# Moving four small reciprocal deviations from ScalarE to Pool in a fused attention and GEGLU kernel

## The chip, the cores and the metric

The kernel runs on one core of a Trainium2 chip. A core has a matmul engine (TensorE, PE in the profile, with its weight loads as PEld), three engines for element-wise work (VectorE as DVE, ScalarE as ACT, GpSimd as POOL) and a sync engine (SP) that issues most DMA transfers. Each engine runs its own queue of instructions in order; an instruction waits on semaphores for what other engines or transfers must have done before it.

The metric is the device time of one execution in microseconds, less is better. The kernel before takes 213.56 us, the median of 3 runs that lie between 213.23 and 213.91 us.

## The reference

The input is one sequence of 2048 rows with 448 columns in bf16. A layer norm without weights feeds two branches, sliding-window attention (16 heads of 28 columns, window 256) and a gated feed-forward layer of width 1792. Their outputs are added to the input.

```python
def _layernorm(x, axis=-1, eps=1e-5):
    m = jnp.mean(x, axis=axis, keepdims=True)
    v = jnp.var(x, axis=axis, keepdims=True)
    return (x - m) / jnp.sqrt(v + eps)

xn = _layernorm(x, axis=-1)
return x + _A_ref(xn, A_wqkv, A_wo) + _B_ref(xn, B_w_gate, B_w_up, B_w_down)
```

The attention branch is a QKV product, masked scores with softmax, the product with V, and the output product with `wo`. The feed-forward branch is `(gelu(x @ w_gate) * (x @ w_up)) @ w_down`.

## The kernel before, in words

The 2048 rows are 16 tiles of 128 rows, one row per partition. Four tiles form a block of 512 rows (`QB`), and the main loop runs over four blocks (`NB`). In each block the scores, their exponentials (L657) and the products with V are interleaved, by a plan written out by hand, with feed-forward products (L457, L391), projections for the next block (L319, L333) and the statistics of later tiles. The order of instructions on each engine is the order of the Python calls (`manual_schedule`); no scheduler moves them.

What the change touches lies ahead of the loop, in the layer norm of the first four tiles. For a tile t:

- `stat(t)` (L155, L156) computes mean and variance of each row on VectorE (`bn_stats`, then the short `bn_aggr`) into `mv_all[:, t, :]`.
- `rstd(t, n)` (L160, L161) turns the variances of n tiles into reciprocal standard deviations in `rstd_all`. It does so on ScalarE in two instructions, Ln of variance plus eps into the work tile `lnv`, then Exp with scale -0.5. One table of ScalarE, loaded at the start (L135), holds both functions and also serves the softmax.
- `norm(t)` (L170) subtracts the mean and multiplies by `rstd_all` on VectorE, giving the bf16 tile `xn`.
- `transp(t, copy, tag)` (L185, L186) transposes it by four small matmuls into the PSUM bank named by `tag`, and copies the result into `xnT`. Tiles 0 and 2 use bank b2, tiles 1 and 3 bank b3; the copies of tiles 0, 1 and 2 run on ScalarE, that of tile 3 on VectorE.

The calls stand in this order (other calls between them left out), and this gives the order of each engine's queue:

```python
warmup(9)
stat(0); rstd(0, 1); stat(1); rstd(1, 1); norm(0)
stat(2); rstd(2, 1); transp(0, nc.scalar.copy, "b2"); norm(1)
stat(3); rstd(3, 1); warmup(1); transp(1, nc.scalar.copy, "b3")
v_dense(0, pvs[0])
norm(2); transp(2, nc.scalar.copy, "b2"); norm(3)
pads(nc.vector.tensor_copy, wqp, slice(0, 1))
transp(3, nc.vector.tensor_copy, "b3")
```

`warmup(n)` (L150) issues n matmuls on zeros (the tile `warm`, cleared by VectorE at L124), which keep PE running while the first loads arrive. `v_dense` (L190) is the dense part of the V product of one tile. Behind the lines shown follow Pool's copy of the last columns of `xnT` (L739), a weight copy on ScalarE (L712), `v_dense(1)`, and the first Q and K products (L190 into `s`), which read all four tiles of `xnT`; then Pool builds the masks (`make_masks`, L117), and VectorE begins tile 4.

Ahead of all this Pool clears two parts of the V tile (L103, L104). `rstd` is called for tile 4, for tiles 5 to 7 together, for 8 to 11 and for 12 to 15 as well. The work tile `lnv` has three buffers in turn.

Of the kernel before, what the change touches and what calls it, by code (L numbers as in the profile page):

```python
# [10 lines left out]
ALU = mybir.AluOpType  # L11
AX = mybir.AxisListType
bf16 = mybir.dt.bfloat16
f32 = mybir.dt.float32
# [3 lines left out]
P = 128  # L18
# [9 lines left out]
def kernel(  # L28
# [11 lines left out]
    nc = tc.nc  # L40
    const = ctx.enter_context(tc.tile_pool(name="const", bufs=1))
# [78 lines left out]

    eps_t = const.tile([P, 1], f32, name="eps_t")
    nc.vector.memset(eps_t[:, :], 1e-5)
    warm = wo[:, :, :].rearrange("p g n -> p (g n)")
    nc.vector.memset(warm[:, 0:QB], 0.0)  # L124
    wqp = const.tile([P, 3, H, 32], bf16, name="wqp")
# [17 lines left out]
    mv_all = const.tile([P, NT, 2], f32, name="mv_all")  # L143
    rstd_all = const.tile([P, NT], f32, name="rstd_all")
# [12 lines left out]

    def rstd(t, n):
        lnv = work.tile([P, 4], f32, name="lnv")
        nc.scalar.activation(out=lnv[:, 0:n], in_=mv_all[:, t:t + n, 1], func=ACT.Ln, bias=eps_t[:, 0:1], scale=1.0)  # L160
        nc.scalar.activation(out=rstd_all[:, t:t + n], in_=lnv[:, 0:n], func=ACT.Exp, scale=-0.5)  # L161

# [555 lines left out]
    warmup(9)  # L718
    stat(0)
    rstd(0, 1)  # L720
    stat(1)
    rstd(1, 1)
    norm(0)
    stat(2)
    rstd(2, 1)
    transp(0, nc.scalar.copy, "b2")
    norm(1)
# [300 lines left out]
```

## Time and profile before

| | |
|---|---|
| median of the runs | 213.56 us |
| the profiled execution, its own time | 213.22 us |
| its span, first to last instruction | 211.5 us |
| mean granted clock of TensorE | 1.000 |
| instructions | 6340 |

The profile is of one execution, and its times count from the span's start. A line of its timeline has start, length, engine, line of the kernel, operation, what it writes and reads, shapes and the number of instructions merged in it; in brackets stands the idle time of the engine ahead of it and what ended it. A line of the chain has start, length, engine and tile. The chain follows the work that ended last back from the end, at each step to what released it. A matmul's length includes its passage through the array, so matmuls in a row overlap and their starts say more than their lengths. Lengths on Pool are rough.

### The profile page before, as it was taken

The page shows a single profiled execution, that of the slowest core. Times are in us where ns is not written, and L with a number is a line of the kernel's source. Part 1 is how long each engine was busy: PE and PEld are TensorE (multiplying, and loading weights), DVE is VectorE, ACT ScalarE, POOL GpSimd, SP SyncE. Part 2 cuts the span into 40 slices and gives each one's busy share as a digit, 9 for nine tenths or more (in the row PEclk, how much of TensorE's full clock was granted, in tenths as well). Part 3 has the DMA queues.
Part 4 walks back from the last instruction along what each step waited for, and adds up shares of the span by engine and source line. Part 5 has one row for each costly group of instructions (what it writes and reads, how often), then busy time and mean ns, then how long its engine had stood idle before and what let it go on. Part 6 is the DMA issues. An engine that isn't in the chain of part 4 may idle for free.

```text
span 211.5 us, 6340 instructions
## 1 busy us (share of the span) xinstructions
PE 206.6 (98%) x2682; PEld 97.4 (46%) x2682; DVE 156.8 (74%) x355; ACT 131.6 (62%) x123; POOL 48.9 (23%) x86
## 2 busy tenths in 40 slices
PE   7999999999999999999999999999999999999994
PEld 2333444444454545444445444544444454544562
DVE  6899988999767985696437897395384699659722
ACT  4699488566677977413778787523577786757000
POOL 5388658451100220041000112013000022005100
PEclk9999999999999999999999999999999999999999
DMA  6999989969410101003521000100100011000011
GB/s 167 289 236 203 108 212 221 220 189 223 111 47 29 39 11 34 9 4 67 74 75 47 25 0 27 22 0 16 31 3 0 10 41 41 7 3 0 22 60 39
DMA packets 24889, 15.67 MB, mean 74 GB/s; under 512 B 9208, under 2 KB 24728, under 8 KB 24856
## 3 DMA queue, kind: packets, MB, share of 16 engines
q1 hardware_dynamic: 23814, 14.87, 32.3%
q8 instruction: 22, 0.36, 0.7%
q10 hardware_dynamic: 1042, 0.34, 0.7%
q14 instruction: 11, 0.09, 0.2%
HBM read 9.26 MB, written 2.41 MB: 55 GB/s over the span
## 4 chain that ended last, share of the span: by engine, by line
PE 94%; DVE 2%; ACT 1%; DMA 1%; issue 0%; DVEq 0%; ACTq 0%
PE po L391 24%; PE gt L457 20%; PE u L457 12%; PE ue L457 8%; PE pq L333 7%; PE sc L653 7%; PE ov L625 5%; PE pv L319 4%; PE pq L190 2%; PE pl L391 2%; DVE st L155 1%; DMA x_sb<-in_A_x_dram 1%; PE pv L190 1%; ACT p_sb L657 1%; PE s L190 1%; PE pk L190 1%
## 5 line engine op out<-in xcount | busy, mean ns | idle before, releaser
L657 ACT ACTIVATE p_sb<-sc 128x2048 bf16<-128x2048 f32 x39 | 73.2, 1878 | 20.6 <-PE sc L653 14.4
L497 ACT ACTIVATE p_sb<-gt 128x1024 bf16<-128x1024 f32 x28 | 28.7, 1024 | 33.7 <-PE gt L457 30.7
L592 POOL TENSOR_TENSOR oN<-oc,l 128x512 bf16<-128x512 f32 x16 | 21.6, 1354 | 119.0 <-DVE l L605 119.0
L457 PE MATMUL gt<-xnT,wg 64*128 64x512 bf16 x224 | 45.6, 376 | 0.0
L391 PE MATMUL po<-wd,hT 128*128 128x448 bf16 x210 | 43.3, 353 | 0.0
L457 PE MATMUL gt<-xsw,wg 64*128 64x512 bf16 x168 | 40.7, 376 | 0.0
L505 DVE TENSOR_TENSOR hT<-p_sb,u 128x512 bf16<-128x512 bf16 x34 | 21.9, 677 | 16.0 <-PE u L457 15.8
L573 DVE TENSOR_TENSOR p_sb<-p_sb,masks 128x256 bf16<-128x256 bf16 (+1 forms) x90 | 27.8, 364 | 7.6 <-ACT p_sb L657 7.6
L391 PEld LDWEIGHTS <-hT 128*128 128x128 bf16 x238 | 21.9, 98 | 19.4 <-issue 2.2
L457 PEld LDWEIGHTS <-wg 64*128 64x128 bf16 x392 | 19.0, 94 | 22.5 <-issue 0.2
L457 PEld LDWEIGHTS <-wu 64*128 64x128 bf16 x392 | 18.8, 94 | 22.4 <-issue 1.0
L457 PE MATMUL u<-xnT,wu 64*128 64x512 bf16 x136 | 28.1, 376 | 0.0
L457 PE MATMUL u<-xsw,wu 64*128 64x512 bf16 x102 | 24.7, 376 | 0.0
L457 PE MATMUL ue<-xnT,wu 64*128 64x512 bf16 x88 | 18.0, 377 | 0.0
L381 DVE TENSOR_TENSOR res<-po,x_sb 128x448 bf16<-128x448 f32 x15 | 9.0, 619 | 11.5 <-PE po L391 11.0
L653 PE MATMUL sc<-qT,kT 28*64 28x320 bf16 (+7 forms) x648 | 16.4, 261 | 0.1
L457 PE MATMUL ue<-xsw,wu 64*128 64x512 bf16 x66 | 16.3, 377 | 0.0
L583 POOL TENSOR_SCALAR_AFFINE_SELECT p_sb<-p_sb 128x512 bf16<-128x512 bf16 (+1 forms) x21 | 14.2, 705 | 5.9 <-ACT p_sb L657 5.8
L610 DVE TENSOR_TENSOR oc<-oc,ov 128x512 f32<-128x512 f32 x12 | 8.2, 681 | 8.6 <-ACT oc L609 8.6
L653 PEld LDWEIGHTS <-kT 28*64 28x64 bf16 (+1 forms) x648 | 7.5, 102 | 13.3 <-issue 12.0
L474 DVE CAST hT<-ue 128x512 bf16<-128x512 f32 x18 | 11.6, 679 | 1.8 <-PE ue L457 1.8
L391 PE MATMUL po<-wo,oN 128*128 128x448 bf16 x54 | 12.0, 352 | 0.0
(110 smaller groups left out, 278.9 us busy)
## 6 DMA issues: line engine op xcount, KB each, us to landing
out_dram<-res SPq DMA_DIRECT2D x15, 112.0 KB
wd<-in_B_w_down_dram SPq DMA_DIRECT2D x2, 784.0 KB
x_sb<-in_A_x_dram SPq DMA_DIRECT2D x3, 448.0 KB
xsw<-xnT SPq DMA_DIRECT2D x6, 192.0 KB
wu<-in_B_w_up_dram SPq DMA_DIRECT2D x4, 224.0 KB
wg<-in_B_w_gate_dram SPq DMA_DIRECT2D x2, 448.0 KB
wu<-in_B_w_up_dram SPq DMA_DIRECT2D x2, 336.0 KB
wg<-in_B_w_gate_dram SPq DMA_DIRECT2D x2, 336.0 KB
```

Of the source, the lines that this page charges most:

```text
L190: nc.tensor.matmul(ps, lhsT=lhs(c), rhs=rhs(c), start=start and c == 0, stop=stop and c == 2, skip_group_check=True)
L333: nc.tensor.matmul(ps, lhsT=w.rearrange("p h d -> p (h d)"), rhs=xchunk(qb, hi, c, qb * QB, QB), start=c == 0, stop=c == 6, tile_position= ...
L391: nc.tensor.matmul(po[:, 0:w], lhsT=x[:, k, tt * P:(tt + 1) * P], rhs=wt[:, k, lo:up], start=start and n == 0, stop=stop and n == len(term ...
L457: nc.tensor.matmul(ps, lhsT=w[64 * hi:64 * hi + 64, c, p * P:(p + 1) * P], rhs=xchunk(qb, hi, c, qb * QB, QB), start=c == 0, stop=c == 6, ...
L474: copy(out=hTs[qb][:, p + 7 * i, :], in_=us[i])
L497: nc.scalar.activation(out=ges[p][:, :, :], in_=gt[:, :, :], func=ACT.Gelu_apprx_tanh)
L505: nc.vector.tensor_tensor(out=hT[:, p + 7 * i, :], in0=ge[:, i, :], in1=u, op=ALU.mult)
L573: nc.vector.tensor_tensor(out=reg, in0=reg, in1=m, op=ALU.mult)
L583: nc.gpsimd.affine_select(out=reg, in_=reg, pattern=mid + [[1 if diag else -1, min(w, P)]], compare_op=ALU.is_ge, fill=0.0, base=0 if diag ...
L592: nc.gpsimd.tensor_tensor(out=oN[:, g, :], in0=oc[:, :], in1=inv, op=ALU.mult)
L653: nc.tensor.matmul(ss[k0:k0 + nk, j, col:col + nq], lhsT=kT[r, g, kt * P + k0:kt * P + k0 + nk], rhs=qT[r, g, ring(qb).start + q0:ring(qb) ...
L657: nc.scalar.activation(out=p_sb[:, :, 0:ncol], in_=ss[:, :, 0:ncol], func=ACT.Exp, scale=SCALE)
```

## The change

For the first four tiles the reciprocal deviation is computed by Pool in two instructions: variance plus eps into `lnv`, then that to the power of a tile that holds -0.5. The tile is cleared to this value by a new memset on VectorE, between those of `eps_t` and `warm`. For tiles 4 to 15 ScalarE's Ln and Exp remain, and its table is loaded as before.

```diff
     eps_t = const.tile([P, 1], f32, name="eps_t")
     nc.vector.memset(eps_t[:, :], 1e-5)
+    minus_half = const.tile([P, 1], f32, name="minus_half")
+    nc.vector.memset(minus_half[:, :], -0.5)
...
     def rstd(t, n):
         lnv = work.tile([P, 4], f32, name="lnv")
+        if t < 4:
+            nc.gpsimd.tensor_scalar(out=lnv[:, 0:n], in0=mv_all[:, t:t + n, 1], scalar1=1e-5, scalar2=None, op0=ALU.add)
+            nc.gpsimd.tensor_tensor(out=rstd_all[:, t:t + n], in0=lnv[:, 0:n], in1=minus_half[:, 0:n], op=ALU.pow)
+            return
         nc.scalar.activation(out=lnv[:, 0:n], in_=mv_all[:, t:t + n, 1], func=ACT.Ln, bias=eps_t[:, 0:1], scale=1.0)
         nc.scalar.activation(out=rstd_all[:, t:t + n], in_=lnv[:, 0:n], func=ACT.Exp, scale=-0.5)
```

On Pool the eight new instructions stand behind the two memsets of the V tile (L103, L104) and ahead of the copy of L739. On ScalarE the eight old ones are gone from ahead of and between the copies of L186. PE's and SP's instructions and their order are the same.

## The prediction

> **What bounds the kernel now.** I read the page's busy shares first, then the waits, then the chain of waits over the first 9 us, since all four replaced pairs lie there.
>
> ```profile
> span 211.5 us, 6340 instructions
> PE 206.6 (98%) x2682; PEld 97.4 (46%) x2682; DVE 156.8 (74%) x355; ACT 131.6 (62%) x123; POOL 48.9 (23%) x86
> ...
> PE wps L150 <- DVE wo L124: 1.4, 1, 1.4
> PE pv L190 <- ACT xnT L186: 0.4, 1, 0.4
> ```
>
> The first two lines are the page's. The last two are every idle stretch that the view of waits gives PE over the first 30 us, and the same view of the whole span has no more of them: 1.42 us until the first warm-up matmul and 0.36 us before the first V product. From there on PE is the bound, and a shift of its start at 8.6 us reaches the end nearly one for one. So the question is whether the start shifts. Lines of the chain there (start, length, work):
>
> ```profile
> 3.58 0.18 DVE mv_all L156
> ...
> 6.38 0.20 DVE mv_all L156
> ...
> 6.60 0.30 ACT lnv L160
> ...
> 6.93 0.20 ACT rstd_all L161
> 7.13 0.48 ACT xnT L186
> ...
> 7.65 0.38 PE tp L185 x4
> ```
>
> Up to 6.58 it runs on VectorE through the statistics of one tile after the other; of ScalarE's pairs only the fourth tile's, 6.60 to 7.13, lies on it. The timeline of the two engines (start, length, engine, line, and idle time in brackets) shows why:
>
> ```profile
> 3.81 0.29 ACT L160 ACTIVATE lnv<-mv_all,eps_t 128x1 f32<-128x1 f32 x1
> 4.14 0.20 ACT L161 ACTIVATE rstd_all<-lnv 128x1 f32<-128x1 f32 x1
> 4.41 0.36 DVE L170 TENSOR_SCALAR xn<-x_sb,mv_all,rstd_all 128x448 bf16<-128x448 bf16 x1
> ...
> 6.00 0.57 ACT L186 COPY xnT<-tp 128x512 bf16<-128x512 bf16 x1
> 6.48 0.37 DVE L170 TENSOR_SCALAR xn<-x_sb,mv_all,rstd_all 128x448 bf16<-128x448 bf16 x1
> 7.04 1.17 ACT L186 COPY xnT<-tp 128x512 bf16<-128x512 bf16 x2
> 7.16 0.40 DVE L170 TENSOR_SCALAR xn<-x_sb,mv_all,rstd_all 128x448 bf16<-128x448 bf16 x1 [0.32 <-ACT rstd_all L161]
> 7.20 0.84 PE L185 MATMUL tp<-ident,xn 128*128 128x128 bf16 x8
> 8.08 0.42 DVE L186 COPY xnT<-tp 128x512 bf16<-128x512 bf16 x1 [0.33 <-PE tp L185]
> 8.56 0.82 PE L190 MATMUL s<-xnT,wqp 128*128 128x512 bf16 x3
> ```
>
> Call X the time from the end of a tile's aggregate to the start of its norm, as far as the pair sets it. For tile 0 the norm could start at 3.76 + 0.65 = 4.41 without moving; tiles 1 and 2 have more room, since VectorE's next statistics lie in between. Tile 3 has none: aggregate done at 6.56, norm at 7.16, X = 0.60, VectorE idle 0.32 us. Behind that norm stand its transposes (7.65), VectorE's copy (8.08) and the Q product (8.56), which needs all four tiles. So X of tile 3 is paid in full, and X of tile 0 from 0.65 on is paid a second time, because tiles 1 to 3 queue behind norm 0 on VectorE.
>
> **The change part by part.** ScalarE loses four pairs of 0.29 + 0.20 us. Its first copy, held until 6.00 by the third pair, can follow the transposes, and its second, now 7.04, can start near 6.3. PE gains nothing by either: the first V product may start some 0.4 us earlier, but PE's order then has the transposes of tiles 2 and 3, and tile 3's wait for norm 3. Today the freed bank (second copy done at 7.61) and norm 3 (7.56) release it together, so with the copy earlier norm 3 alone decides, 0.03 us sooner. That is ScalarE's whole contribution, a gain of 0.03.
>
> Pool gains two instructions per tile, in its queue behind the two memsets of the V tile and ahead of the copy at 8.67:
>
> ```profile
> 1.01 0.06 DVE L122 MEMSET eps_t<- 128x1 f32 x1
> ...
> 2.92 0.63 DVE L155 BATCH_NORM_STATS2 st<-x_sb 128x6 f32<-128x448 bf16 x1 [0.90 <-DMA x_sb<-in_A_x_dram]
> ...
> 1.42 3.94 PE L150 MATMUL wps<-wo 128*128 128x512 bf16 x9 [1.42 <-DVE wo L124]
> 5.20 0.39 PE L185 MATMUL tp<-ident,xn 128*128 128x128 bf16 x4
> 5.87 0.40 PE L185 MATMUL tp<-ident,xn 128*128 128x128 bf16 x4
> ...
> 2.14 1.52 POOL L104 MEMSET v_sb<- 128x768 bf16 x1
> 8.67 0.61 POOL L739 COPY xnT<-xnT 64x512 bf16<-64x512 bf16 x1 [5.01 <-ACT wkp L712]
> ```
>
> Pool is free from 3.66, before the first aggregate at 3.76, and idle for 5.01 us: nothing that is queued behind the new waits is wanted before tile 3's copy (8.50), which comes after the last new instruction. The added memset of the exponent costs 0.06 us on VectorE, inside its 0.90 us wait for the first tile. It delays the warm-up matmuls by as much; the nine end near 5.36 and tile 0's transposes start at 5.20 among them, but nobody waits for these before tile 1's at 5.87. Nothing there; 0.06 if that cover were gone. No DMA is added or moved.
>
> Now the price of a Pool pair. Rows for small Pool instructions and for how Pool is woken (by line and form: busy, mean ns; by line: min/median/max ns; the timeline):
>
> ```profile
> L283 POOL COPY wqp<-wraw 128x16 bf16<-128x16 bf16 x3 | 0.6, 190 | 0.0
> L1012 POOL MEMSET const-float32-0.0<- 128x1 f32 x1 | 0.1, 103 | 0.3 <-issue 0.3
> ...
> L592 POOL TENSOR_TENSOR oN<-oc,l x16: 1264/1270/1719, 32.8 to 194.3; 128x512 bf16<-128x512 f32 x16
> ...
> L117 POOL TENSOR_SCALAR_AFFINE_SELECT masks<-masks x18: 232/237/359, 9.3 to 14.3; 64x64 bf16<-64x64 bf16 x18
> ...
> 76.06 0.70 DVE L605 STREAM_TRANSPOSE l<-inv_all 128x512 f32<-128x512 f32 x1
> 76.85 1.27 POOL L592 TENSOR_TENSOR oN<-oc,l 128x512 bf16<-128x512 f32 x1 [4.84 <-DVE l L605]
> ...
> 12.61 0.38 DVE L170 TENSOR_SCALAR xn<-x_sb,mv_all,rstd_all 128x448 bf16<-128x448 bf16 x1
> 12.71 0.36 POOL L117 TENSOR_SCALAR_AFFINE_SELECT masks<-masks 64x64 bf16<-64x64 bf16 x1
> ```
>
> Wake by VectorE: 76.76 to 76.85, so 0.08 to 0.09. The addition is nearest to the 16-column copy: 0.19. Between dependent instructions 0.04, as between ScalarE's two (4.10 to 4.14). From Pool to VectorE I take the same 0.04. The addition of tiles 1 to 3 starts while VectorE runs the norm of the tile before (6.48 to 6.85 against 6.64). A mask instruction that started 0.10 us into a norm took 0.36 in place of the median 0.237: 0.12 more. A gain by such a neighbour is excluded.
>
> The Trainium skill says the same more sharply in "SBUF — State Buffer", section "SBUF: two separate sides": whichever of a GpSimd instruction and a VectorE one in a two-port mode starts first holds the shared port pair to its end, and the other is fully blocked. By that rule the addition of tile 3 would run only after 6.85 and end at 7.04, against 6.95 by the row: 0.09 more in the sum. The row agrees that there is a charge, but the mask instruction ended 0.08 after the norm, not its own 0.237.
>
> The power p has no row. Lower end: the 128x1 memset, 0.10. Upper end: a whole two-input instruction of 512 columns, 1.27. One column is nearest to the small rows, 0.19, but a general power is more work per column than a copy, so I take 0.45, a quarter of the way from 0.19 to 1.27.
>
> Sum with p: X of tile 0 is 0.08 + 0.19 + 0.04 + p + 0.04 = 0.35 + p, of tile 3 with the neighbour's 0.12 it is 0.47 + p. At p = 0.45: norm 0 is late by 0.80 - 0.65 = 0.15, norm 3 by a further 0.92 - 0.60 = 0.32, less the 0.03 of the freed bank: **+0.44 us** (in general 2p - 0.46 for p above 0.30, and p - 0.16 below). Against the profiled execution, 213.22 us with 1.7 us outside its span, that is 213.66; that execution is 0.34 under the median of the runs, so 214.0 by the median, 0.2% up. A measurement of this kernel cannot tell 0.3%, 0.64 us, from no change.
>
> **The rivals.**
>
> *A pair no slower than ScalarE's.* With both instructions at the memset's 0.11 and no neighbour's charge, X is 0.38, norm 3 starts at 6.94, and the gain is 0.22 + 0.03 = 0.25: 213.3. More than about 0.34 is not there, since norm 2 ends at 6.85 and VectorE's 0.32 us of idling is all that tile 3 can give back. For it: Pool idles there, and the chain shows ScalarE's pair. Against it: two instructions at 0.19 with the wake already make 0.54 before any power is computed.
>
> *The power is slow and Pool becomes the chain (slower).* Place: the four pairs in Pool's queue. It decides beyond noise from p = 0.55, where 2p - 0.46 reaches 0.64, and from about p = 0.72 the pairs wait for each other. At p = 1.27 the four take 4 x (0.19 + 0.04 + 1.27) and three gaps of 0.04 from 3.84 on, so norm 3 starts at 10.0 in place of 7.16: +2.8, or 216.4. For it: no Pool row of this profile computes anything but moves, selects and products, and a product of 512 columns already takes 1.27. Against it: only one column.
>
> *The first power pays a load of its code.* Place: tile 0's power; tiles 1 to 3 queue behind norm 0, so all of it is paid. The only load with a row is ScalarE's table, and by it +0.44 + 1.28, or 215.3. Against it: Pool's first two-input instruction follows its predecessor's end (32.84) at once and takes the median.
>
> ```profile
> 2.52 1.28 ACT L135 ACT_TABLE_LOAD   x1 [2.52 <-DVE masks L134]
> ...
> 31.02 1.82 POOL L583 TENSOR_SCALAR_AFFINE_SELECT p_sb<-p_sb 128x512 bf16<-128x512 bf16 x3 [0.80 <-ACT p_sb L657]
> 32.81 1.27 POOL L592 TENSOR_TENSOR oN<-oc,l 128x512 bf16<-128x512 f32 x1
> ```
>
> "GPSIMD Engine Reference" of the Trainium skill, section "Instruction dispatch", puts the first call of freshly loaded Pool code at about 6 us with no instruction to show for it; by that figure the time would be an estimated 220 us. No row here shows such a gap.
>
> **How the numbers follow.** Forecast (p from 0.25 to 0.55) 0.43; no slower pair 0.15, of which 0.05 are counted as faster beyond noise in case later stages add to it; slow power 0.38; code load 0.04. Faster 0.05, same 0.43 + 0.10 + 0.02 of the slow power's lower edge = 0.55, slower 0.40. The time is the forecast's, 214.0. The range goes from 213.2 (the fastest pair, with the scatter of the runs) to 216.2, just short of p = 1.27; the code load and a power above that row are left out. The forecast's own range is 213.5 to 214.3.
>
> **What would show it.** Right: in the new profile norm 3 starts at 7.4 to 7.8, idle before it by Pool; the first copy of ScalarE starts near 5.7 and the second before 7.0 with no effect; the Q product starts 0.3 to 0.7 later than 8.56; PE's busy time is unchanged, and the shift found at 9 us stands at the end. Wrong: two power instructions starting more than 0.9 us apart with Pool busy between them (slow power); a first pair much longer than the others (code load); norm 3 before 7.16 (fast pair); or a difference at the end that isn't there at 9 us, which would put the cause in a stage that I take as untouched.

## The result and the profile after

The changed kernel takes 214.07 us (median of 9 runs, 214.00 to 214.35), the kernel before in runs beside it 213.43 (9 runs, 213.18 to 213.91): a ratio of 1.0031, with a 95% interval from 1.0023 to 1.0040. The change costs 0.64 us, 0.5 to 0.85 by the interval. That it is slower is certain; whether by more than 0.3% is not, since that bound lies in the middle of the interval.

The chain of waits of the changed kernel over the first 9 us (start, length, work; lines of the changed kernel are up to 6 higher):

```profile
2.87 0.64 DVE st L157
...
3.73 0.08 issue
3.81 0.24 POOL lnv L163
4.04 0.07 issue
4.12 0.58 POOL rstd_all L164
4.69 0.03 issue
4.72 0.40 DVE xn L176
...
6.91 0.08 issue
6.99 0.37 POOL lnv L163
7.35 0.07 issue
7.42 0.58 POOL rstd_all L164
8.00 0.03 issue
8.03 0.41 DVE xn L176
8.44 0.05 issue
8.48 0.40 PE tp L191 x4
```

Two of Pool's pairs lie on it, the first tile's and the fourth's, where the kernel before had one of ScalarE's. Each is read off whole: 0.08 until Pool starts, the addition, 0.07 between the two, the power, 0.03 to VectorE. From the aggregate's end the first pair takes 3.71 to 4.72, 1.01 us, the fourth 6.90 to 8.03, 1.13 us. In the kernel before norm 0 could wait 0.65 us for its pair without moving, and tile 3's pair took 0.60 on ScalarE. The timeline shows the wait on VectorE and what stands behind it:

```profile
4.72 0.40 DVE L176 TENSOR_SCALAR xn<-x_sb,mv_all,rstd_all 128x448 bf16<-128x448 bf16 x1 [0.25 <-POOL rstd_all L164]
...
5.82 0.58 ACT L192 COPY xnT<-tp 128x512 bf16<-128x512 bf16 x1 [2.03 <-PE tp L191]
...
6.46 0.74 PE L196 MATMUL pv<-wv,xnT 128*128 128x448 bf16 x3
6.64 0.59 ACT L192 COPY xnT<-tp 128x512 bf16<-128x512 bf16 x1 [0.24 <-PE tp L191]
...
8.03 0.40 DVE L176 TENSOR_SCALAR xn<-x_sb,mv_all,rstd_all 128x448 bf16<-128x448 bf16 x1 [0.72 <-POOL rstd_all L164]
...
9.40 0.82 PE L196 MATMUL s<-xnT,wqp 128*128 128x512 bf16 x3
9.45 0.62 DVE L157 BATCH_NORM_STATS2 st<-x_sb 128x6 f32<-128x448 bf16 x1
...
11.26 0.69 DVE L250 CAST kT<-s 128x512 bf16<-128x512 f32 x1 [0.24 <-PE s L202]
...
12.01 0.40 PE L659 MATMUL sc<-qT,kT 28*128 28x128 bf16 x8
```

ScalarE's copies start earlier, 5.82 and 6.64 in place of 6.00 and 7.04, and the first V product 0.16 earlier, to no use: norm 3 is 0.87 late, the Q product 0.84, and the first score matmul 0.84 (12.01 against 11.17 before). From there to the end of the span there are 200.4 us after and 200.3 before, so the shift is carried to the end unchanged. The profiled execution of before, 213.22, is one of that kernel's faster ones, so the two profiles differ by 0.85 us and the medians by 0.64.

The Pool instructions by line and form (busy us, mean ns), where the kernel before had none:

```profile
L164 POOL TENSOR_TENSOR rstd_all<-lnv,minus_half 128x1 f32<-128x1 f32 x4 | 2.3, 570 | 0.3
L163 POOL TENSOR_SCALAR lnv<-mv_all 128x1 f32<-128x1 f32 x4 | 1.1, 269 | 0.7 <-DVE mv_all L158 0.4
```

### The profile page after: what moved, and what is told of

Its sections match the earlier page's. It is cut to its first block, busy times and chain, and to the rows that moved or that the text cites. A ratio compares the mean times of both kernels' runs of the same rounds, so it can differ in the third digit from the quotient of the medians.

```text
span 212.4 us, 6343 instructions
## 1 busy us (share of the span) xinstructions
PE 206.8 (97%) x2682; PEld 97.4 (46%) x2682; DVE 157.0 (74%) x356; ACT 129.8 (61%) x115; POOL 52.2 (25%) x94
## 4 chain that ended last, share of the span: by engine, by line
PE 94%; DVE 2%; DMA 1%; ACT 1%; POOL 1%; issue 1%; DVEq 0%; ACTq 0%
PE po L397 24%; PE gt L463 20%; PE u L463 12%; PE ue L463 8%; PE pq L339 7%; PE sc L659 6%; PE ov L631 5%; PE pv L325 4%; PE pq L196 2%; PE pl L397 2%; DMA x_sb<-in_A_x_dram 1%; PE pv L196 1%; ACT p_sb L663 1%; DVE st L157 1%; PE s L196 1%; PE pk L196 1%
```

## The experiments

Below, "over before" is the difference of medians against runs of the kernel before on the same chip, with the ratio's 95% interval; times of single instructions are from each run's profile.

**Tile 3's pair back on ScalarE.**

```diff
-        if t < 4:
+        if t < 3:
```

> The changed kernel, but tile 3's pair back on ScalarE; tiles 0 to 2 stay on Pool. Theory (both ends of the queue pay: tile 0's pair delays norm 0 and all behind it on VectorE, tile 3's is paid again): tile 3's X falls from 1.13 back to 0.60, norm 0 stays near 4.72, so the Q product starts near 8.56 + 0.33 = 8.9 and the time is about 0.3 us over that of before. Rival (only tile 3's wait counts, tile 0's lateness is absorbed by the slack further on): Q product near 8.56, time as before. A middle value of 0.1 or less would speak for the rival.

213.72 us against 213.37, 0.35 over before (ratio 1.0016, 1.0007 to 1.0025). Norm 0 starts at 4.74, norm 3 at 7.59, the Q product at 8.98. The lateness of norm 0 is not absorbed.

**Only tile 3's pair on Pool.**

```diff
-        if t < 4:
+        if t == 3:
```

> The changed kernel with only tile 3's pair on Pool; tiles 0 to 2 back on ScalarE. Theory: norm 0 back at 4.41, norm 3 at 6.56 + 1.13 = 7.69, Q product near 9.1, time about 0.5 us over before, so that this and the run with tile 3 alone on ScalarE add up to the whole loss. Rival (only tile 3's wait counts): the whole loss stays, 0.65 to 0.85 us.

213.75 us against 213.37, 0.38 over before (1.0019, 1.0009 to 1.0029). Norm 0 starts at 4.47, norm 3 at 7.72, the Q product at 9.09. So either end pays: 0.35 + 0.38 = 0.73, beside 0.64 for the whole, and both rivals fall. This end costs less than the 0.5 expected. Here the first load came 0.06 later than in the first profile of before, which these starts contain.

**A multiplication for the power.**

```diff
-            ... in1=minus_half[:, 0:n], op=ALU.pow)
+            ... in1=minus_half[:, 0:n], op=ALU.mult)
```

> Pool's second instruction multiplies by -0.5 in place of raising to the power -0.5 (tiles 0 to 3 are then scaled wrongly), all else as in the changed kernel. Theory (the power itself is the mis-sized term): the second instruction takes about 0.2 in place of 0.57, X of tile 0 falls to 0.64 and of tile 3 to 0.76, norm 0 is back at 4.41, norm 3 near 7.3, the Q product near 8.7, the time 0.1 to 0.2 us over before. Rival (waking Pool, its dispatch and the port that it shares with VectorE make the loss): the second instruction still takes 0.4 or more or the gaps stay, Q product at 9.1 or later, time at least 0.4 us over before.

213.41 us against 213.37, no difference (1.0001, 0.9992 to 1.0010). The timeline of Pool in this run:

```profile
3.86 0.21 POOL L163 TENSOR_SCALAR lnv<-mv_all 128x1 f32<-128x1 f32 x1 [0.20 <-DVE mv_all L158]
4.15 0.19 POOL L164 TENSOR_TENSOR rstd_all<-lnv,minus_half 128x1 f32<-128x1 f32 x1
...
6.65 0.26 POOL L163 TENSOR_SCALAR lnv<-mv_all 128x1 f32<-128x1 f32 x1 [0.50 <-DVE mv_all L158]
6.99 0.19 POOL L164 TENSOR_TENSOR rstd_all<-lnv,minus_half 128x1 f32<-128x1 f32 x1
```

The same instruction with another operation takes 0.19 in place of 0.57. All else is left as it was: the wakes, the gaps, the second instruction, the memset. Norm 0 starts at 4.41, norm 3 at 7.22, the Q product at 8.59, a little better than expected, since the addition beside norm 2 took 0.26 and not 0.355. The power's own 0.38 us, twice, is what decides; the dispatch on Pool alone costs about what ScalarE's pair did.

**The power alone, without eps.**

```diff
-            nc.gpsimd.tensor_scalar(out=lnv[:, 0:n], in0=mv_all[:, t:t + n, 1], scalar1=1e-5, scalar2=None, op0=ALU.add)
-            nc.gpsimd.tensor_tensor(out=rstd_all[:, t:t + n], in0=lnv[:, 0:n], in1=minus_half[:, 0:n], op=ALU.pow)
+            nc.gpsimd.tensor_tensor(out=rstd_all[:, t:t + n], in0=mv_all[:, t:t + n, 1], in1=minus_half[:, 0:n], op=ALU.pow)
```

> Pool raises the variance itself to the power -0.5 in one instruction; the addition of eps is left out for tiles 0 to 3. Theory (X is the sum of wake, addition, gaps and power): X falls by the addition and one gap, about 0.3, in tile 0 to about 0.70 and in tile 3, where the power now starts beside norm 2, to 0.7 to 0.8; norm 0 near 4.45, norm 3 near 7.3, Q product near 8.7, time 0.1 to 0.3 us over before. Rival (the power alone makes the loss, the addition is hidden): time as that of the changed kernel.

213.72 us against 213.41 (1.0011, 1.0002 to 1.0020): slower than before, and less so than the changed kernel, as the theory has it. Norm 0 starts at 4.40, norm 3 at 7.30, the Q product at 8.68. The profiled execution took 213.40, near the low end of this kernel's 213.28 to 213.92, and its Q product is only 0.12 later than before; where the other 0.19 of the 0.31 between the medians comes from is not shown. In Pool's timeline the first power stands alone and the others beside a norm of VectorE:

```profile
3.81 0.55 POOL L163 TENSOR_TENSOR rstd_all<-mv_all,minus_half 128x1 f32<-128x1 f32 x1 [0.16 <-DVE mv_all L158]
4.54 0.67 POOL L163 TENSOR_TENSOR rstd_all<-mv_all,minus_half 128x1 f32<-128x1 f32 x1 [0.17 <-DVE mv_all L158]
...
6.66 0.61 POOL L163 TENSOR_TENSOR rstd_all<-mv_all,minus_half 128x1 f32<-128x1 f32 x1 [0.43 <-DVE mv_all L158]
```

The neighbour costs 0.06 to 0.12 us, and each of the three ends 0.41 after the norm that it began beside.

**Only tiles 1 and 2 on Pool.**

```diff
-        if t < 4:
+        if t in (1, 2):
```

> Only tiles 1 and 2 on Pool, tiles 0 and 3 on ScalarE. Theory (tiles 1 and 2 have slack on VectorE of 0.3 us or more): norm 3 at 7.16 as before, Q product 8.5 to 8.6, time as before within 0.1 us; ScalarE's first copy comes earlier and brings nothing. Rival (every Pool pair costs, by its wake or by the port that it shares with VectorE): 0.2 us or more over before.

213.49 us against 213.41 (1.0004, 0.9995 to 1.0013): as before within the interval. But norm 3 starts at 7.39 and the Q product at 8.79, not at 7.16 and 8.5 to 8.6. VectorE's timeline has norm 1, tile 3's aggregate and norm 3 so:

```profile
5.58 0.40 DVE L176 TENSOR_SCALAR xn<-x_sb,mv_all,rstd_all 128x448 bf16<-128x448 bf16 x1
...
6.55 0.18 DVE L158 BATCH_NORM_AGGREGATE mv_all<-st 128x2 f32<-128x6 f32 x1
...
7.39 0.40 DVE L176 TENSOR_SCALAR xn<-x_sb,mv_all,rstd_all 128x448 bf16<-128x448 bf16 x1 [0.29 <-ACT rstd_all L167]
```

The first load came 0.04 later here. Norm 1 starts directly behind tile 1's power (4.98 + 0.56), at 5.58 in place of 5.45; tile 3's statistics queue behind it, and their aggregate starts at 6.55 in place of 6.38. ScalarE, idle by then, begins tile 3's pair 0.10 after that aggregate in place of 0.04. Norm 2 is late too (6.71, behind tile 2's power), but norm 3 waits for ScalarE and not for it. The room of tiles 1 and 2 in the kernel before is 5.45 - 4.49 = 0.96 and 6.48 - 5.53 = 0.95 us; here their Pool pairs take 1.05 and 1.15. The middle tiles are not quite free either; of that only the bound of 0.13% at the end can be told. In the changed kernel norm 1 does not wait for its pair: with norm 0 late, it starts at 5.78 straight behind VectorE's own statistics.

**No pair at all.**

```diff
+    nc.vector.memset(rstd_all[:, 0:4], 20.0)
...
         if t < 4:
-            nc.gpsimd.tensor_scalar(out=lnv[:, 0:n], in0=mv_all[:, t:t + n, 1], scalar1=1e-5, scalar2=None, op0=ALU.add)
-            nc.gpsimd.tensor_tensor(out=rstd_all[:, t:t + n], in0=lnv[:, 0:n], in1=minus_half[:, 0:n], op=ALU.pow)
             return
```

> No pair at all for tiles 0 to 3: their reciprocal deviation is a constant written by one VectorE memset at the start (these tiles are then scaled wrongly). This gives the most that any faster pair could win. Theory: VectorE never waits between its statistics and norms, norm 3 starts at 6.85, the Q product near 8.25, time 0.3 us under before. Rival (PE's order, the banks or the loads hold the start anyway): Q product not before 8.45, time as before within 0.1.

213.35 us against 213.37 (0.9998, 0.9989 to 1.0007): nothing is won. VectorE runs norms 2 and 3 back to back from 6.56 to 7.23, as the theory had it, and yet the Q product starts at 8.64 and the first score matmul at 11.39, later than before. That is the rival, as far as it names the loads. The Q product stands behind a first V product that waited 0.30 us for the V weights and started at 6.95 in place of 6.62; the scores wait for another load. The chain of this run (start, length, work) does not go through the layer norm of the first four tiles at all:

```profile
4.78 4.39 DMA x_sb<-in_A_x_dram
...
9.19 0.64 DVE st L158
...
9.85 0.18 DVE mv_all L159
10.03 0.52 DVE st L158
...
10.58 0.18 DVE mv_all L159
10.76 0.59 DVE kT L249
...
11.39 0.42 PE sc L658 x8
```

It begins with the load of tiles 4 to 7. That lands near 9.17; VectorE's queue has the statistics of tiles 4 and 5 ahead of the first K copy, and the first scores wait for that copy. In the first profile of before these statistics start at 8.83 without a wait, and the K copy, at 10.42, follows both them and PE's product within 0.1 us. In a second profile of the kernel before (213.18 us) the load is already the later one:

> The kernel before once more, for a second profile. If late V weights make part of its spread (213.17 to 214.06 us), the first V product shows a wait for a transfer in some executions; the first profile shows none, with the product at 6.62. Expected here: the first V product between 6.6 and 7.0, the Q product between 8.55 and 8.9, and the time over 213.22 by the difference.

```profile
8.55 0.82 PE L190 MATMUL s<-xnT,wqp 128*128 128x512 bf16 x3
8.95 0.63 DVE L155 BATCH_NORM_STATS2 st<-x_sb 128x6 f32<-128x448 bf16 x1 [0.26 <-DMA x_sb<-in_A_x_dram]
9.71 0.59 DVE L155 BATCH_NORM_STATS2 st<-x_sb 128x6 f32<-128x448 bf16 x1
...
10.44 0.67 DVE L244 CAST kT<-s 128x512 bf16<-128x512 f32 x1
```

The first V product is at 6.62 again, without a wait for a transfer; the wait is elsewhere than expected. So two paths of the kernel before end at the K copy within 0.1 us of each other, and shortening the layer norm alone has no room.

**The loads: V weights first, without a pair and with ScalarE's.** I first took the wait of 0.30 us for the V weights in the run without a pair for the new bound. The run with the power alone has one as well (0.44 us, until 6.72), without effect there, since norm 3 comes later.

```diff
+    nc.sync.dma_start(out=wv[:, 0:3, :], in_=rows(A_wqkv, 0, 3)[:, :, 2 * D:3 * D])
     for c in (0, D):
-        nc.scalar.dma_start(out=wraw[:, 0:3, c:c + 4 * Dh], in_=wqk[:, :, c:c + 4 * Dh])
-    nc.sync.dma_start(out=wv[:, 0:3, :], in_=rows(A_wqkv, 0, 3)[:, :, 2 * D:3 * D])
+        nc.sync.dma_start(out=wraw[:, 0:3, c:c + 4 * Dh], in_=wqk[:, :, c:c + 4 * Dh])
```

> The run without any pair, with the V weights issued ahead of the two first parts of the raw Q and K weights (these move from ScalarE's queue to SP's, behind them). In the run without a pair PE waited 0.30 us for the V weights ahead of the first V product, which started at 6.95. Theory (the load of the V weights took the place of the removed pair): the first V product starts near 6.5 without a wait for a transfer, the transposes of tiles 2 and 3 follow, the Q product starts near 8.3, and the time is 0.3 us under before. Rival (something else at the start holds it: the clock that PE gets after its warm-up, or the raw weights, now later): Q product at 8.5 or later and no gain over before.

> The kernel before with the same change of the loads and ScalarE's pairs untouched. Theory: norm 3 stays at 7.16 behind ScalarE's pair, so the Q product stays at 8.5 to 8.6 and the time at that of before within 0.1 us, with a smaller spread if the late V weights made part of it. Rival (the V weights bound the kernel before, too): Q product 0.2 us or more earlier and the time with it.

Without a pair: 214.00 us against 213.37 (1.0029, 1.0018 to 1.0040); with ScalarE's pairs: 213.96 against 213.37 (1.0033, 1.0020 to 1.0047). Both times are missed. The first V product starts at 6.57 and 6.68 without a wait for a transfer, and the Q product at 8.61 in both, beside 8.56 before. With ScalarE's pairs that is where the theory had it; without a pair it is the rival's side, and there the first V product itself ran slowly (last section). But the two loads that moved to SP's queue make the issue of tiles 4 to 7 a microsecond later, 5.84 in place of 4.78, and the chain of the run with ScalarE's pairs shows what that does:

```profile
5.84 3.77 DMA x_sb<-in_A_x_dram
...
9.63 0.64 DVE st L155
...
11.20 0.59 DVE kT L244
...
11.83 0.43 PE sc L653 x8
```

The first scores start 0.66 later than before, 11.83, with the same Q product, and the time rises by 0.59.

**The same loads, tile 5's statistics behind the K copy.**

```diff
     rstd(4, 1)
-    stat(5)
     qk_halves(0, 0, pq, pk)
...
+    stat(5)
     for dst in (wqp, wkp):
         pads(nc.vector.tensor_copy, dst, slice(2, 4))
```

> The run with the V weights first and ScalarE's pairs, with one more call moved: the statistics of tile 5 go on VectorE behind the first K copy and the next weight copies. In the run with the V weights first the Q product started at 8.61, as before, but the time rose by 0.6 us; the load of tiles 4 to 7 came later, tile 4's statistics waited 0.88 us for it, and the K copy queued behind the statistics of tiles 4 and 5 until 11.12, the first score matmul until 11.83. Theory (this load, through VectorE's queue, is the second bound of the start, and the reason why the run without a pair won nothing): the K copy starts at 10.4 to 10.5 right behind PE or tile 4's statistics, the first score matmul at 11.2 to 11.3, and the time falls back to 213.3 to 213.5. Rival (the rise comes from other loads that the changed order made late): K copy earlier but the first score matmul or the end not, time still 213.9 or more.

213.74 us against 213.39 (1.0018, 1.0009 to 1.0027): between theory and rival. The K copy starts at 10.47, as expected, but the first score matmul only at 11.64. ScalarE's timeline shows the second way in which the load holds the scores:

```profile
10.59 0.29 ACT L160 ACTIVATE lnv<-mv_all,eps_t 128x1 f32<-128x1 f32 x1 [2.06 <-DVE mv_all L156]
10.91 0.20 ACT L161 ACTIVATE rstd_all<-lnv 128x1 f32<-128x1 f32 x1
11.02 0.57 ACT L243 CAST qT<-s 128x512 bf16<-128x512 f32 x1
```

Tile 4's pair, which waits for that tile's statistics, stands ahead of the first Q copy on ScalarE. The load reaches the scores through the queues of both engines, and one call moved frees one of them.

**Tile 3's statistics ahead of norm 1**, with ScalarE's pairs and with Pool's:

```diff
-    norm(1)
     stat(3)
+    norm(1)
     rstd(3, 1)
```

> The kernel before with one call moved: norm(1) after stat(3), so that VectorE has two norms to run while ScalarE does tile 3's pair. Theory: VectorE's 0.32 us of idling ahead of norm 3 goes away, norm 3 starts near 6.85, Q product near 8.25, time 0.3 us under before. Rival (the later transposes of tile 1 and their bank hold the start): Q product at 8.5 or later, no gain.

> The changed kernel with the same call moved (norm(1) after stat(3)). Theory: norm 0 stays at 4.72; tile 3's aggregate ends 0.3 us earlier than in the changed kernel, about 6.6, Pool's pair for it ends near 7.7 in place of 8.0, and the two norms lie beside it; Q product near 9.1, time about 0.3 us under the changed kernel and 0.4 over before. Rival (Pool's pairs hold each other up, or the shared port does): no better than the changed kernel.

With ScalarE: 213.44 us against 213.41 (1.0006, 0.9997 to 1.0015), no gain; norm 3 starts at 7.11, not 6.85, since ScalarE's pair now stands behind its first copy. The Q product is at 8.64 even so: PE's transposes of tile 1 waited 0.89 us for the later norm 1 and started at 6.67 in place of 5.87, and the first V product behind them at 6.91 in place of 6.62. That is the rival, as to the transposes. Tile 4's load was waited for, too (0.38 us). With Pool: 213.98 against 213.41 (1.0025, 1.0012 to 1.0037), that is 0.57 over before beside 0.64 for the changed kernel, where I expected 0.3 us under it: Pool's pair for tile 3 waited for tile 2's power, which ran until 7.09, and its own power took 0.66 beside a norm. This much of the rival is right. The Q product starts at 9.36, but in this profile the first load came 0.18 later than in that of the changed kernel (first statistics at 3.05 and 2.87), which 9.36 contains; how much the order would win without that is open.

## Why the prediction was right, and where it was not

**What bounds the start.** Right for the direction asked: the shift at the Q product, 0.84, is found at the first scores and at the end of the span. In the profiles of all these runs the first score matmul and the end lie 200.3 to 200.4 us apart. Not right was that PE is the bound from the first V product on: behind the Q product VectorE waits for tiles 4 to 7 (not at all and 0.26 us in the two profiles of before, 0.41 without a pair), and that path ends at the K copy together with PE's. I had read PE's waits alone, and there it leaves no mark.

**Two payments.** Right, and shown by the two runs that divide the change: 0.35 us with tiles 0 to 2 on Pool, which is tile 0's lateness, and 0.38 with tile 3 alone.

**The signs.** Norm 3 at 8.03 and a Q product 0.84 late lie outside what the prediction named as signs of being right (7.4 to 7.8, and 0.3 to 0.7), on the side of a slower power. The others came: ScalarE's earlier copies without effect, PE's busy time unchanged (206.6 and 206.8 us), the shift of 9 us found at the end. No sign of being wrong did: Pool is idle between those powers that start more than 0.9 us apart.

**The power.** The forecast took 0.45, a quarter of the way between the two bounds; it measured 0.57. This is the term that was mis-sized, and it counts twice, 0.24 us. Of the other terms three were a little short (wake 0.10 for 0.08, addition 0.23 for 0.19, gap 0.08 for 0.04) and the hand-over a little long (0.03 for 0.04), together 0.09 in X, and again twice. So 0.44 + 0.24 + 0.18 = 0.86, beside 0.84 in the profile. That the forecast by the median, 214.0, is so near to the measured 214.07 is in part luck, of two kinds. It started from 213.56, the median of three runs; from the 213.43 of nine it would have been 213.87. And the shift between the medians, 0.64, is smaller than the 0.85 between the profiles. A likely reason for the second is that an execution of before in which tiles 4 to 7 land late loses time that the changed kernel, whose scores come later, has covered. Its runs spread by 0.35 us, those of before by 0.73. The two fastest executions, 214.00 and 213.18, lie 0.82 apart, as the profiles do, which fits; but no execution of before from the upper part of its spread was profiled, so this is argued, not shown.

**The neighbour's 0.12.** The size is right, in part by luck. The fourth addition took 0.355 beside norm 2, the first 0.23 alone:

```profile
6.91 0.40 DVE L176 TENSOR_SCALAR xn<-x_sb,mv_all,rstd_all 128x448 bf16<-128x448 bf16 x1
6.99 0.35 POOL L163 TENSOR_SCALAR lnv<-mv_all 128x1 f32<-128x1 f32 x1
```

The prediction had the addition begin 0.16 us into the norm (6.64 against 6.48). Where it does so, in the run with the multiplication (6.65 against 6.48), it takes 0.26 in place of 0.21, a charge of 0.05. In the changed kernel tile 2's power, which ran until 6.88, held norm 2 back, so that the addition began only 0.08 into it. In the runs with a Pool pair every addition that began 0.07 to 0.17 us into a norm ended 0.03 to 0.09 after that norm, and one that began 0.27 into it (6.80 against 6.53, only tile 3 on Pool) took 0.23, as if alone. So the charge depends on how far into the norm Pool begins.

The stricter form that the prediction weighed from the Trainium skill ("SBUF — State Buffer", section "SBUF: two separate sides", the other engine fully blocked) would have let that addition begin at norm 2's end, 7.31; it ended at 7.34. With its whole 0.23 behind the norm it would have ended at 7.54, so the measured charge is the smaller one. That Pool gets through the first part of its instruction and is then held until the norm ends would fit these rows; no run tests it.

**ScalarE's relief.** Right that it brings next to nothing: its copies came 0.18 and 0.40 us earlier, and from norm 3 to the Q product it is 1.37 us in place of 1.40, the 0.03 of the forecast.

**The rivals.** The slow power was rightly placed and priced: its point of decision, p = 0.55, is where the measurement came out, at the edge of 0.3%. Whether the change belongs to this rival's "slower" or to the forecast's "same" the interval leaves open; a change from none it does tell, which the prediction had doubted for 0.64 us. At 0.57 it is the forecast's own mechanism with the larger value, and the chain does not run through Pool's queue. One pair does wait there: tile 1's addition starts at 4.66, 0.19 after its aggregate, behind tile 0's power. The prediction's p = 0.72 for such waiting overlooked that tile 1's aggregate follows only 0.73 us after tile 0's (4.49 and 3.76), which by its own terms gives 0.46. It costs nothing, since norm 1 starts later anyway. No code load: the first power took 0.57 like the others. The rival of a pair no slower than ScalarE's was wrong in its worth. Its 0.25 us, and the 0.34 that I named as the most, aren't there: with the pair removed altogether the time is that of before (the interval leaves a gain of 0.23 us at the most), since another path is as long.

## What to carry to other kernels

When a small step moves to another engine, its price is the whole path from producer to consumer, with wake, gaps and hand-over, and it is paid once for each place in the queue where the consumer has no room; read that room off the consumer's idle time first. To learn what a step could give at best, run the kernel without it: here the answer was nothing, because a load and two queues behind it ended at the same point. Here a path that ended within a tenth of a microsecond of another left no mark in PE's waits, and showed only when the first was shortened.

## What the runs showed of the hardware that was not expected

A power of one column on Pool takes 0.57 us where a product of the same shape takes 0.19. Between dependent instructions Pool leaves 0.08 us by the timeline, twice ScalarE's 0.04.

TensorE's speed at the start is not the same in all the profiled executions, though the mean granted clock is 0.999 to 1.000 in all of them. In the run without a pair and with the V weights first, the first V product ran slower than the second of the same shape:

```profile
6.57 1.07 PE L195 MATMUL pv<-wv,xnT 128*128 128x448 bf16 x3
...
7.93 0.73 PE L195 MATMUL pv<-wv,xnT 128*128 128x448 bf16 x3
```

That took back 0.34 of the 0.38 us by which it started earlier than in the run without a pair and with the loads unchanged; what sets the moment at which the matmuls become faster was not tried.
